# Attention and gated feed-forward on one core: products with v in one step, splits in four parts, first weights loaded earlier

## The chip, the cores and the metric

The kernel runs on one core of a Trainium2 chip. The metric is the device time of one execution in microseconds. Five engines work side by side, each through its own queue in order: TensorE (PE) multiplies and transposes, VectorE (DVE), ScalarE (ACT) and GpSimd (POOL) do the elementwise work, and SyncE (SP) issues most of the DMA transfers; POOL issues some itself. PEld in a profile is PE's loading of weights, which overlaps its multiplying.

## The reference

Two parts follow each other, all in float32:

```
scores = q k^T / 8 + bias[h]                 # 4 batches, 8 heads, 576 positions, 64 wide
bias   = relu(x w1 + b1) w2,  x = log1p(|i - j|) / log1p(max(i, 1))
attn   = softmax(scores);  out = attn v       # heads side by side: 2304 tokens x 512
h = out w_in                                  # 512 -> 2048
y = (h * tanh(softplus(h))) w_out             # 2048 -> 512
```

## The kernel before, in words

The bias stage comes first. It makes the bias for 16 positions at a time (36 tiles, `idx` 0 to 35), writes each tile to DRAM (`bias_d`), and reads whole bias blocks of a head pair back (`load_bias`).

The attention stage works through 16 pairs. A pair is one batch element with two heads, and it has five steps, one for each chunk of query rows in `ORDER = [0, 1, 4, 2, 3]`. Chunks 0 to 3 hold 128 rows of each head, chunk 4 the last 64 rows of both. `step(n)` writes the order of the work of step n by hand; n = 5i + x, with x the place in the pair. The work of a chunk is spread over several steps:

- `scores` (L218): q k^T in two PSUM tiles of 128x576. Each product is taken with q as a rounded high part (`hi`) and with the remainder (`q_lo`); the remainder of k lies in the lower half of `hi`.
- `add_bias` (L234, VectorE): adds the bias, finds the row extremes. `exps` (L249, ScalarE): exponential and row sums. For chunk 4 a 64-column copy follows on POOL (L252), which the last transpose of that chunk (L300) reads.
- `transposes` (L283 to L302), two steps later: PE turns the chunk, ScalarE copies it out of PSUM into `main` and `tail`. The PSUM tiles (`t_ps`) are three.
- `pv_duo(i, grp, k)` (L315 to L324): one of the five products with v of a group. Group 0 holds chunks 0 and 1, group 1 chunks 4, 2 and 3. The five add up in one PSUM tile `o`, of which there is one. VectorE copies it (L327) and SP stores it to `x_d` (L329 to L332).

The five products of a group are spread over three steps for group 0 (x = 4, then 0 and 1 of the next pair) and two for group 1 (x = 2 and 3 of the next pair), always behind the transposes of the step.

For the next pair, `load_hi` (L170, POOL's queue) loads q and k with rounding and `load_raw` (L161 to L164, SP's queue) loads them as they are, with v. `hi` has two buffers, raw has one. On POOL `split_k` (L175) and `split_q` (L180) subtract the one from the other, each as one instruction of 64x1216. Both loads are issued in the first step of the pair before.

Beside this the weights of the feed-forward part are loaded two at a time (`load_weights`, L105) and converted in four pieces each, L119 or L117, L122, L124 and L126, one or two pieces per step, mostly on VectorE. When a weight is done the next is loaded. For the first four weights POOL also does a subtraction (L137).

The feed-forward stage follows (L593 and L631): per block of tokens three passes of the first product, the gate, three passes of the second.

Of the kernel before, what the change touches and what calls it, by code (L numbers as in the profile page):

```python
# [7 lines left out]
F32 = mybir.dt.float32  # L8
# [3 lines left out]
ALU = mybir.AluOpType  # L12
# [3 lines left out]
B, H, S, D, C = 4, 8, 576, 64, 32  # L16
# [5 lines left out]
QW = 1216  # L22
# [24 lines left out]
def kernel(ctx: ExitStack, tc, qk, v, wb, w2, w_in, w_out, psia, psi4, rinv, eye, out):  # L47
# [122 lines left out]
        pool.dma_start(out=hi, in_=qk[b, hp])  # L170
        qk_hi[i] = hi

    def split_k(i):
        kl = qk_hi[i][64:128, QW:]
        (pool if i else dve).tensor_tensor(kl, qk_raw[i][64:128], kl.bitcast(F32), op=ALU.subtract)  # L175

    def split_q(i):

        lo = q_los[i % 2]
        (pool if i else dve).tensor_tensor(lo[0:64], qk_raw.pop(i)[0:64], qk_hi[i][0:64, :QW].bitcast(F32), op=ALU.subtract)  # L180
        q_lo[i] = lo

    def load_bias(hp, c):
# [55 lines left out]
    def exps(n, u):  # L239

        i, c = steps[n]
        if u == 1 and c == 4:
            return
        if i not in sums:
            sums[i] = st.tile([P, 9], F32, name="sums", bufs=3)
        pt, m = live[n]
        ps = pt[:, u * S:(u + 1) * S]
        k = 4 * u + c if c < 4 else 8
        act.activation(ps, ps, AF.Exp, bias=m[:, u:u + 1], scale=-1.0, accum_out=sums[i][:, k:k + 1])  # L249
        if c == 4:  # L250

            pool.tensor_copy(pt[:, S:640], pt[:, 512:S])  # L252

    def reciprocals(i):

# [48 lines left out]
    def pv_duo(i, grp, k):  # L304
        hp, b = divmod(i, B)
        main, tail = pt_t[i, grp]
        vt = v_t[i]
        w = 256 if grp == 0 else 320
        if k == 0:
            o_t[0] = o_ps.tile([P, 512], F32, name="o")  # L310
        o = o_t[0]
        kw = dict(skip_group_check=True)
        if k < 4:
            for h in range(2):
                pe.matmul(o[h * 64:h * 64 + 64, :w], vt[:, h, k, :], main[:, h, k, :],  # L315
                          start=(k == 0), stop=False, **kw)
            return
        if grp == 0:
            for h in range(2):
                pe.matmul(o[h * 64:h * 64 + 64, :w], vt[:, h, 4, :], tail, start=False, stop=True, **kw)  # L320
        else:
            pe.matmul(o[0:64, :w], vt[:, 0, 4, :], tail[:, 0:320], start=False, stop=True, **kw)
            pe.matmul(o[64:128, 64:320], vt[:, 1, 4, :], tail[:, 64:320], start=False, stop=True, **kw)
            pe.matmul(o[64:128, 0:64], vt[:, 1, 4, :], tail[:, 320:384], start=False, stop=True, **kw)  # L324
        del pt_t[i, grp]
        x = xs.tile([P, 320], F32, name="x")
        dve.tensor_copy(x[:, :w], o[:, :w])  # L327
        if grp == 0:
            sp.dma_start(out=x_d[b][:, hp, 0:256], in_=x[:, :256])  # L329
        else:  # L330
            sp.dma_start(out=x_d[b][:, hp, 256:512], in_=x[:, 64:320])
            sp.dma_start(out=x_d[b][:, hp, 512:576], in_=x[:, 0:64])  # L332
# [49 lines left out]
    def split(n):  # L382

        i, x = divmod(n, 5)
        if (x == 1 or n == 3) and i + 1 < NPAIR:
            split_k(i + 1)
        if x == 3 and i + 1 < NPAIR:
            split_q(i + 1)

        for _ in range((2, 2, 2, 1, 2)[x]):  # L390
            if not conv and w64:
                conv.append(conv_weights(x == 2))
            elif conv and next(conv[0]):
                conv.clear()
                load_weights()
                if w32[0][0] in order[:EARLY]:
                    split_weights(pool)

    def step(n):
        i, x = divmod(n, 5)  # L400
        late = n == 4

        def begin():
            if n < NS:
                scores(n)
                add_bias(n)
                exps(n, 0)

        def end():
            if n < NS:  # L410
                exps(n, 1)
                ahead(n)
            if 0 <= n - 1 < NS and (n - 1) % 5 == 4:
                rc[n - 1] = reciprocals((n - 1) // 5)
            if n < NS:
                split(n)


        if not late:
            begin()  # L420
        for k in {3: (0, 1)}.get(n, (n - LAG,)):
            if 0 <= k < NS:
                transposes(k)
        if not late:
            end()

        if late:
            for k in range(5):
                pv_duo(0, 0, k)
        for j, grp, ks in {4: ((i, 0, (0, 1)),), 0: ((i - 1, 0, (2, 3)),), 1: ((i - 1, 0, (4,)),),  # L430
                           2: ((i - 1, 1, (0, 1, 2)),), 3: ((i - 1, 1, (3, 4)),)}[x]:
            if 0 <= j < NPAIR and (j, grp) != (0, 0):
                for k in ks:
                    pv_duo(j, grp, k)
        if late:
            begin()
            end()

# [74 lines left out]
    for idx in range(NB + 2):  # L515
# [25 lines left out]
            load_raw(1)  # L541
        if idx == 18:
            load_hi(1)
    bias_scope.close()

    ptp = lsbuf("ptp", 1)
    xs = lsbuf("xs", 2)
    load_weights()
    x0 = lsbuf("x0")
    o_ps = lpsum("o_ps", 1)  # L550
    t_ps = lpsum("t_ps", 3)
# [105 lines left out]
    hidden(*units[0])  # L657
    step(NS + 1)
    step(NS + 2)
    step(NS + 3)  # L660
    left_scope.close()

    wq = sbuf("wq")
# [82 lines left out]
```

## Time and profile before

| what | value |
|---|---|
| median of 3 runs | 769.67 us (769.43 to 774.86) |
| the profiled execution | 776.47 us, its span 774.7 us |
| PE busy | 723.3 us, 93% of the span |
| VectorE, ScalarE, POOL busy | 68%, 59%, 14% |
| mean granted clock of PE | 0.977 |
| chain that ended last, by line | L631 and L593 24% each; load of raw q and k 4%; scores, products with v, bias loads 3% each |

The times are those of whole executions. A profile shows one execution, taken by itself; its span runs from its first to its last instruction, and its time is given beside it because sums over rows belong to that execution and not to the median. Busy shares are averages over stages with different limits: attention runs from about 60 to 357 us, the feed-forward stage from there to the end.

### The profile page before, as it was taken

What the parts mean: (1) busy time and instruction counts of PE and PEld (TensorE: products, weight loads), DVE (VectorE), ACT (ScalarE), POOL (GpSimd) and SP (SyncE); (2) the same over time, 40 slices, a digit from 0 to 9 for tenths busy, and PEclk for the clock granted to TensorE, in tenths of its full rate; (3) what the DMA queues carried; (4) which work ended last, traced back from release to release, by engine and by line L of the source; (5) the groups of instructions that cost most, each with busy time, mean ns of one, the idle gap of its engine ahead of it and who ended that gap; (6) DMA issues with size and microseconds to landing.
All of it is one profiled execution on the core that took longest, in us unless ns stands there. A gap on an engine that the chain in (4) does not pass through costs nothing.

```text
span 774.7 us, 11579 instructions
## 1 busy us (share of the span) xinstructions
PE 723.3 (93%) x4160; PEld 553.0 (71%) x4160; DVE 525.1 (68%) x1047; ACT 459.5 (59%) x982; POOL 110.9 (14%) x76
## 2 busy tenths in 40 slices
PE   6688989899988998979999999999999999999997
PEld 3226667676766676756888888888987888888886
DVE  7974788678857876744977856656557566665554
ACT  6986777677756776746766644444444554444443
POOL 1003443333332334350000000000000000000000
PEclk9989999999989999989999999999999999999999
DMA  8988469876975697820400003000410500010001
GB/s 280 297 282 278 121 207 316 211 238 189 320 213 165 200 320 227 252 52 16 117 1 2 0 20 90 0 1 1 129 35 1 136 0 1 1 55 1 1 0 55
DMA packets 45610, 93.60 MB, mean 121 GB/s; under 512 B 13408, under 2 KB 22256, under 8 KB 43504
## 3 DMA queue, kind: packets, MB, share of 16 engines
q1 hardware_dynamic: 42672, 72.70, 32.0%
q0 software_dynamic: 2304, 19.92, 7.8%
q8 instruction: 33, 0.54, 0.3%
q10 hardware_dynamic: 576, 0.22, 0.1%
q14 instruction: 25, 0.20, 0.1%
HBM read 72.43 MB, written 20.40 MB: 120 GB/s over the span
## 4 chain that ended last, share of the span: by engine, by line
PE 57%; DMA 16%; DVE 8%; ACT 5%; POOL 3%; issue 2%; SPq 2%; DVEq 0%; POOLq 0%; ACTq 0%
PE y L631 24%; PE h L593 24%; DMA rawqk<-in_qk_dram 4%; PE s L218 3%; PE o L315 3%; DMA bias<-bias_d 3%; DMA w<-in_w_out_dram 3%; DVE pt L234 2%; PE tp L283 2%; POOL qkhi L175 1%; ACT pt L249 1%; DMA w<-in_w_in_dram 1%; DMA vt<-in_v_dram 1%; ACT main L284 1%; DMA qkhi<-in_qk_dram 1%
## 5 line engine op out<-in xcount | busy, mean ns | idle before, releaser
L249 ACT ACTIVATE pt<-pt,m 128x576 f32<-128x576 f32 x144 | 112.8, 784 | 90.5 <-DVE m L234 90.5
L234 DVE CUSTOM_DVE_ANT_0 pt<-s,bias 128x576 f32<-128x576 f32 x144 | 103.8, 752 | 38.9 <-PE s L218 38.1
L631 PE MATMUL y<-who,ghi 128*128 128x512 f32 x288 | 113.8, 395 | 0.2 <-ACT ghi L615 0.2
L631 PE MATMUL y<-who,glo 128*128 128x512 f32 x288 | 113.9, 396 | 0.0
L631 PE MATMUL y<-wlo,ghi 128*128 128x512 f32 x288 | 113.7, 395 | 0.0
L615 ACT CAST ghi<-e 128x512 fp32r<-128x512 f32 x72 | 44.7, 621 | 89.9 <-DVE e L611 89.8
L315 PE MATMUL o<-main,vt 128*64 128x320 f32 (+1 forms) x512 | 79.8, 436 | 8.1 <-DVE x L327 8.0
L598 ACT ACTIVATE e<-h 128x512 f32<-128x512 f32 x72 | 42.9, 598 | 71.4 <-PE h L593 71.4
L218 PE MATMUL s<-qkhi 128*128 128x288 f32 x320 | 79.2, 330 | 3.9 <-issue 2.7
L599 DVE TENSOR_SCALAR e<-e 128x512 f32<-128x512 f32 x72 | 30.7, 426 | 76.2 <-ACT e L598 76.2
L593 PE MATMUL h<-xhi,whi 128*128 128x512 f32 (+1 forms) x320 | 81.0, 373 | 0.8 <-ACT xhi L575 0.7
L593 PE MATMUL h<-xlo,whi 128*128 128x512 f32 (+1 forms) x320 | 80.4, 372 | 0.9 <-DVE xlo L577 0.8
L593 PE MATMUL h<-xhi,wli 128*128 128x512 f32 (+1 forms) x320 | 80.0, 371 | 0.0
L616 DVE TENSOR_TENSOR glo<-e,ghi 128x512 fp32r<-128x512 f32 x72 | 49.7, 690 | 43.8 <-ACT ghi L615 43.8
L218 PE MATMUL s<-qkhi,qlo 128*128 128x288 f32 x320 | 71.0, 304 | 6.3 <-POOL qlo L180 6.3
L218 PEld LDWEIGHTS s<-qkhi 128*128 128x128 f32 x320 | 51.5, 195 | 32.5 <-issue 22.0
L283 PE MATMUL tp<-ident,pt 128*128 128x128 f32 x512 | 69.6, 281 | 1.0 <-ACT main L284 0.9
L284 ACT COPY main<-tp 128x512 f32<-128x512 f32 x128 | 67.7, 578 | 0.7 <-PE tp L283 0.5
L593 PEld LDWEIGHTS h<-xhi,whi 128*128 128x128 f32 x320 | 57.2, 188 | 14.1 <-ACT xhi L575 2.1
L593 PEld LDWEIGHTS h<-xlo,whi 128*128 128x128 f32 x320 | 56.8, 188 | 12.9 <-DVE xlo L577 1.7
L593 PEld LDWEIGHTS h<-xhi,wli 128*128 128x128 f32 x320 | 56.8, 188 | 11.3
L631 PEld LDWEIGHTS y<-who,glo 128*128 128x128 f32 x288 | 54.1, 188 | 13.7 <-DVE glo L616 0.9
(75 smaller groups left out, 1160.6 us busy)
## 6 DMA issues: line engine op xcount, KB each, us to landing
qkhi<-in_qk_dram POOLq DMA_DIRECT2D x16, 1216.0 KB, 7.7
bias_d<-bt SPq DMA_DIRECT2D x36, 295.5 KB
rawqk<-in_qk_dram SPq DMA_DIRECT2D x32, 304.0 KB
w<-in_w_in_dram SPq DMA_DIRECT2D x16, 512.0 KB
w<-in_w_out_dram SPq DMA_DIRECT2D x16, 512.0 KB
vt<-in_v_dram SPq DMA_DIRECT2D x16, 320.0 KB
bias<-bias_d SPq DMA_DIRECT2D x16, 288.0 KB
out_dram<-w SPq DMA_DIRECT2D x17, 256.0 KB
```

Of the source, the lines that this page charges most:

```text
L218: pe.matmul(s[:, j, :SH], stat[:, q0:q0 + P], hi[:, QW + kc + j * SH:QW + kc + (j + 1) * SH], start=(k == 0), stop=(k == len(todo) - 1))
L234: dve.tensor_tensor_reduce(out=halves(pt[:, sl]), in0=s[:, :, :SH], in1=halves(bt[:, sl]), scale=-0.125, scalar=BIG, op0=ALU.add, op1=ALU. ...
L249: act.activation(ps, ps, AF.Exp, bias=m[:, u:u + 1], scale=-1.0, accum_out=sums[i][:, k:k + 1])
L283: pe.transpose(tp[:, k * P:(k + 1) * P], pt[:, c0:c0 + P], ident)
L284: act.copy(main[:, h, :, off:off + P], tp.rearrange("p (k q) -> p k q", k=4))
L315: pe.matmul(o[h * 64:h * 64 + 64, :w], vt[:, h, k, :], main[:, h, k, :], start=(k == 0), stop=False, **kw)
L593: pe.matmul(h[:, u * n:(u + 1) * n], w["i", g4, d][:, r * P:(r + 1) * P], x[:, d, :n], start=(k == 0), stop=(k == 11))
L598: act.activation(e, h, AF.Exp)
L599: dve.tensor_scalar(e, e, E20, None, op0=ALU.min)
L615: act.copy(ghi, e)
L616: dve.tensor_tensor(glo, e, ghi.bitcast(F32), op=ALU.subtract)
L631: pe.matmul(ys[blk][t], g[:, c0:c0 + P], w, start=(f == 0 and k == 0), stop=(f == NFC - 1 and k == 2))
```

## The change: what it does

Five edits go together. (1) `step` runs the five products of a group in one step: group 0 at x = 4, group 1 at x = 2 of the next pair, the step after the last transposes of the group. They stand behind the scores and ahead of the transposes of that step; step 4, the first with products, keeps its own order. (2) VectorE's copy and the stores become a function of their own, `store_x`, at the end of that step. (3) From the second split on, `split_k` and `split_q` are four instructions of 64x304 each; their places in the program are x = 1 and 2 for k and x = 3 and 4 for q. (4) The 64-column copy of chunk 4 is made on ScalarE, behind its exponential. (5) The first call of `load_weights` stands at `idx` 26 of the bias stage.

```diff
--- before.py
+++ after.py
@@ -170,14 +170,21 @@
         pool.dma_start(out=hi, in_=qk[b, hp])
         qk_hi[i] = hi
 
-    def split_k(i):
-        kl = qk_hi[i][64:128, QW:]
-        (pool if i else dve).tensor_tensor(kl, qk_raw[i][64:128], kl.bitcast(F32), op=ALU.subtract)
-
-    def split_q(i):
+
+    QPART = QW // 4
+
+    def split_k(i, parts=range(4)):
+        for r in parts if i else (slice(0, QW),):
+            r = r if i == 0 else slice(r * QPART, (r + 1) * QPART)
+            kl = qk_hi[i][64:128, QW:][:, r]
+            (pool if i else dve).tensor_tensor(kl, qk_raw[i][64:128, r], kl.bitcast(F32), op=ALU.subtract)
+
+    def split_q(i, parts=range(4)):
 
         lo = q_los[i % 2]
-        (pool if i else dve).tensor_tensor(lo[0:64], qk_raw.pop(i)[0:64], qk_hi[i][0:64, :QW].bitcast(F32), op=ALU.subtract)
+        for r in parts if i else (slice(0, QW),):
+            r = r if i == 0 else slice(r * QPART, (r + 1) * QPART)
+            (pool if i else dve).tensor_tensor(lo[0:64, r], qk_raw[i][0:64, r], qk_hi[i][0:64, r].bitcast(F32), op=ALU.subtract)
         q_lo[i] = lo
 
     def load_bias(hp, c):
@@ -249,7 +256,7 @@
         act.activation(ps, ps, AF.Exp, bias=m[:, u:u + 1], scale=-1.0, accum_out=sums[i][:, k:k + 1])
         if c == 4:
 
-            pool.tensor_copy(pt[:, S:640], pt[:, 512:S])
+            act.copy(pt[:, S:640], pt[:, 512:S])
 
     def reciprocals(i):
 
@@ -323,6 +330,11 @@
             pe.matmul(o[64:128, 64:320], vt[:, 1, 4, :], tail[:, 64:320], start=False, stop=True, **kw)
             pe.matmul(o[64:128, 0:64], vt[:, 1, 4, :], tail[:, 320:384], start=False, stop=True, **kw)
         del pt_t[i, grp]
+
+    def store_x(i, grp):
+        hp, b = divmod(i, B)
+        w = 256 if grp == 0 else 320
+        o = o_t[0]
         x = xs.tile([P, 320], F32, name="x")
         dve.tensor_copy(x[:, :w], o[:, :w])
         if grp == 0:
@@ -382,10 +394,16 @@
     def split(n):
 
         i, x = divmod(n, 5)
-        if (x == 1 or n == 3) and i + 1 < NPAIR:
-            split_k(i + 1)
-        if x == 3 and i + 1 < NPAIR:
-            split_q(i + 1)
+        if i + 1 < NPAIR:
+            if n == 3:
+                split_k(1)
+                split_q(1)
+            elif i and x == 1:
+                split_k(i + 1, (0, 1))
+            elif i and x == 2:
+                split_k(i + 1, (2, 3))
+            elif i and x >= 3:
+                split_q(i + 1, ((0, 1), (2, 3))[x - 3])
 
         for _ in range((2, 2, 2, 1, 2)[x]):
             if not conv and w64:
@@ -416,25 +434,29 @@
                 split(n)
 
 
+        pv = [(j, grp) for at_x, j, grp in ((4, i, 0), (2, i - 1, 1)) if x == at_x and 0 <= j < NPAIR]
+
+        def products():
+            for j, grp in pv:
+                for k in range(5):
+                    pv_duo(j, grp, k)
+
+        def turn():
+            for k in {3: (0, 1)}.get(n, (n - LAG,)):
+                if 0 <= k < NS:
+                    transposes(k)
+
+
+        if late:
+            turn()
+            products()
+        begin()
         if not late:
-            begin()
-        for k in {3: (0, 1)}.get(n, (n - LAG,)):
-            if 0 <= k < NS:
-                transposes(k)
-        if not late:
-            end()
-
-        if late:
-            for k in range(5):
-                pv_duo(0, 0, k)
-        for j, grp, ks in {4: ((i, 0, (0, 1)),), 0: ((i - 1, 0, (2, 3)),), 1: ((i - 1, 0, (4,)),),
-                           2: ((i - 1, 1, (0, 1, 2)),), 3: ((i - 1, 1, (3, 4)),)}[x]:
-            if 0 <= j < NPAIR and (j, grp) != (0, 0):
-                for k in ks:
-                    pv_duo(j, grp, k)
-        if late:
-            begin()
-            end()
+            products()
+            turn()
+        end()
+        for j, grp in pv:
+            store_x(j, grp)
 
 
 
@@ -541,11 +563,12 @@
             load_raw(1)
         if idx == 18:
             load_hi(1)
+        if idx == 26:
+            load_weights()
     bias_scope.close()
 
     ptp = lsbuf("ptp", 1)
     xs = lsbuf("xs", 2)
-    load_weights()
     x0 = lsbuf("x0")
     o_ps = lpsum("o_ps", 1)
     t_ps = lpsum("t_ps", 3)
@@ -657,7 +680,6 @@
     hidden(*units[0])
     step(NS + 1)
     step(NS + 2)
-    step(NS + 3)
     left_scope.close()
 
     wq = sbuf("wq")
```

How the order on the engines changes shows in three places. PE before, from the third step of a pair (first row) through its fifth: `s` are scores, `tp` transposes, `o` products, and 952 is the group 1 of the pair before, 1096 group 0 of this pair.

```order
L218 MATMUL s<-qkhi,qlo_117 128x288 x2
L283 MATMUL tp<-ident,pt 128x128 x8
L286 MATMUL tp<-ident,pt 128x128
L315 MATMUL o<-main_952,vt 64x320 x6
L218 MATMUL s<-qkhi 128x288 x2
...
L286 MATMUL tp<-ident,pt 128x128
L315 MATMUL o<-main_952,vt 64x320 x2
L322 MATMUL o<-tail_953,vt 64x320
...
L300 MATMUL tp<-ident,pt_1092 128x128
L315 MATMUL o<-main_1096,vt 64x256 x4
L218 MATMUL s<-qkhi 128x288 x2
```

The same stretch of PE in the changed kernel (958 is group 1 of the pair before, 1115 group 0 of this pair):

```order
L225 MATMUL s<-qkhi,qlo_117 128x288 x2
L322 MATMUL o<-main_958,vt 64x320 x8
L329 MATMUL o<-tail_959,vt 64x320
...
L290 MATMUL tp<-ident,pt 128x128 x8
...
L225 MATMUL s<-qkhi,qlo_117 128x288 x2
L322 MATMUL o<-main_1115,vt 64x256 x8
L327 MATMUL o<-tail_1116,vt 64x256 x2
L303 MATMUL tp<-ident,pt_1099 128x128 x4
L307 MATMUL tp<-ident,pt_1099 128x128
L225 MATMUL s<-qkhi 128x288 x2
```

All products of a group now stand between the scores and the transposes of one step, and none are left for the steps after it. The second place is POOL, one split and the load behind it, before:

```order
L175 TENSOR_TENSOR qkhi<-rawqk,qkhi 64x1216
L252 COPY pt_1535<-pt_1535 128x64
L180 TENSOR_TENSOR qlo_116<-rawqk,qkhi 64x1216
L170 DMA qkhi<-in_qk_dram 128x2432
L175 TENSOR_TENSOR qkhi<-rawqk,qkhi 64x1216
```

and in the changed kernel:

```order
L180 TENSOR_TENSOR qkhi<-rawqk,qkhi 64x304 x4
L187 TENSOR_TENSOR qlo_116<-rawqk,qkhi 64x304 x4
L170 DMA qkhi<-in_qk_dram 128x2432
L180 TENSOR_TENSOR qkhi<-rawqk,qkhi 64x304 x4
L187 TENSOR_TENSOR qlo_117<-rawqk,qkhi 64x304 x4
```

The copy is gone from POOL, and the load still stands behind the last part. The third place is SP, from the stores of one group 1 to the next raw load, before (`rawqk` is raw, `r_d` the reciprocals of the row sums):

```order
L329 DMA x_d_83<-x 128x256
L105 DMA w_1782<-in_w_out_dram 128x1024
L331 DMA x_d_83<-x 128x256
L332 DMA x_d_83<-x 128x64
L161 DMA rawqk<-in_qk_dram 64x1216
```

and in the changed kernel:

```order
L105 DMA w_1821<-in_w_out_dram 128x1024
L343 DMA x_d_83<-x 128x256
L344 DMA x_d_83<-x 128x64
L341 DMA x_d_80<-x 128x256
L161 DMA rawqk<-in_qk_dram 64x1216
```

The store of group 0 of the running pair (L341) now stands directly ahead of the raw load, where before the stores of group 1 of the pair before stood.

## Rows read from the trace of the kernel before

**Rows 1.** View by stretches: PE, PEld, DVE, ACT, POOL busy, granted clock, DMA share, GB/s.
```profile
60.00:350.00 290.00, 262.74 (x1856) 198.49 (x1856) 206.19 (x465) 197.63 (x512) 107.39 (x68) 0.95 0.73 219
400.00:425.00 25.00, 25.00 (x109) 20.12 (x108) 19.67 (x34) 16.49 (x29) 0.00 (x0) 1.00 0.00 1
```

**Rows 2.** Waits of PE in 60 to 350: total us, times, longest.
```profile
PE tp L300 <- POOL pt L252: 8.8, 5, 3.2
PE o L315 <- DVE x L327: 7.1, 10, 2.7
PE s L218 <- POOL qlo L180: 6.3, 5, 3.8
PE s L218 <- issue: 2.7, 1, 2.7
```

**Rows 3.** Timeline of POOL, one ordinary turn: start, us, line, [idle before].
```profile
147.53 0.57 POOL L170 DMA_DIRECT2D qkhi<-in_qk_dram  x1
158.28 2.79 POOL L175 TENSOR_TENSOR qkhi<-rawqk,qkhi 64x1216 fp32r<-64x1216 f32 x1 [10.18 <-DMA rawqk<-in_qk_dram]
161.13 0.24 POOL L252 COPY pt<-pt 128x64 f32<-128x64 f32 x1
161.32 2.79 POOL L180 TENSOR_TENSOR qlo<-rawqk,qkhi 64x1216 fp32r<-64x1216 f32 x1
164.06 0.57 POOL L170 DMA_DIRECT2D qkhi<-in_qk_dram  x1
```

**Rows 4.** Timeline of POOL: first and last of twelve issues, and two prices.
```profile
76.43 1.28 POOL L137 TENSOR_TENSOR wli<-w,whi 128x512 fp32r<-128x512 f32 x1 [7.59 <-ACT whi L136]
...
109.72 0.57 POOL L170 DMA_DIRECT2D qkhi<-in_qk_dram  x1
...
124.36 0.58 POOL L252 COPY pt<-pt 128x64 f32<-128x64 f32 x1
...
314.00 0.57 POOL L170 DMA_DIRECT2D qkhi<-in_qk_dram  x1
```

**Rows 5.** Waits of all engines in 60 to 350.
```profile
POOL qkhi L175 <- DMA rawqk<-in_qk_dram: 128.2, 11, 14.7
```

**Rows 6.** Timeline, late turns: POOL and PE.
```profile
215.93 2.74 POOL L175 TENSOR_TENSOR qkhi<-rawqk,qkhi 64x1216 fp32r<-64x1216 f32 x1 [14.71 <-DMA rawqk<-in_qk_dram]
...
219.10 0.33 PE L300 MATMUL tp<-ident,pt 128*128 128x128 f32 x1 [3.19 <-POOL pt L252]
...
337.21 0.85 PE L218 MATMUL s<-qkhi,qlo 128*128 128x288 f32 x2 [3.79 <-POOL qlo L180]
```

**Rows 7.** Timeline of DVE, PE and POOL around 235.
```profile
231.69 3.17 DVE L124 SCALAR_TENSOR_TENSOR w<-w,w 128x512 uint32<-128x512 uint32 x1
...
235.24 1.84 PE L315 MATMUL o<-main,vt 128*64 128x320 f32 x12 [2.69 <-DVE x L327]
...
236.90 0.24 POOL L252 COPY pt<-pt 128x64 f32<-128x64 f32 x1 [2.59 <-ACT pt L249]
...
242.12 0.57 POOL L170 DMA_DIRECT2D qkhi<-in_qk_dram  x1 [2.25 <-PE s L218]
```

**Rows 8.** View by stretches: the clock after two stalls.
```profile
70.00:74.00 4.00, 3.38 (x16) 3.39 (x17) 3.93 (x13) 2.64 (x7) 0.00 (x0) 0.57 0.94 352
335.00:345.00 10.00, 7.79 (x39) 6.30 (x40) 4.02 (x9) 3.30 (x8) 4.65 (x3) 0.66 0.23 53
```

**Rows 9.** Chain of waits (start, us), timeline of DVE and PE: first weights.
```profile
63.80 5.27 DMA w<-in_w_in_dram
...
69.09 0.43 DVE L119 TENSOR_SCALAR w<-w 128x512 f32<-128x512 f32 x1 [7.44 <-DMA w<-in_w_in_dram]
...
70.62 0.82 PE L218 MATMUL s<-qkhi 128*128 128x288 f32 x2 [2.66 <-issue]
```

**Rows 10.** Timeline of PE: products of group 0 in three places.
```profile
168.10 1.08 PE L315 MATMUL o<-main,vt 128*64 128x256 f32 x8
...
171.46 0.65 PE L320 MATMUL o<-tail,vt 128*64 128x256 f32 x4
```

## The prediction

> **What bounds the kernel now.** The first view to read is the one by stretches. It cuts the program in two. In 400 to 425 TensorE (PE) is busy for 25.00 of 25.00 us: the feed-forward part is bound by PE, its work and order stay as they are, and it is worth nothing here. In 60 to 350, the attention part, PE is busy for 262.74 of 290 us, so it idles for 27.3, and its granted clock is 0.95, which takes another 5% of 290, or 14.5 us [rows 1]. Together 42 us is the most that any reordering of attention can give.
>
> The view of waits says who ends those idle times [rows 2]: 8.8 us for the 64-column copy that POOL makes in the third chunk of a pair (L252), 7.1 us for VectorE's copy of the products out of their one PSUM buffer (L327), 6.3 us for POOL's split of q (L180), and one gap of 2.7 us marked "issue". Three of the four are touched by the change, so 18.6 us look like a sure gain.
>
> The third view, POOL's timeline, says why they are not. One turn of POOL reads [rows 3]: issue of the load of the next pair's q and k (147.53), wait of 10.18 for the second, raw copy of them, split of k (2.79), the small copy, split of q (2.79), and at once the next issue (164.06). There is one raw buffer, so the next raw load needs this split's end as well. **This is a loop of its own**: load, split, load. From the first to the last of the twelve issues from 109.72 to 314.00 there are eleven turns in 204.28 us, 18.57 each [rows 4]. Of each, 0.57 is the issue, the wait for raw is 128.2 / 11 = 11.65 on average [rows 5], and 6.35 are left for the splits and what stands between them. So where PE waits for POOL, PE is waiting for this loop. The turn at 215.93 shows it: raw lands 14.71 us after POOL came free, and only then can the copy follow for which PE has been idle 3.19 us [rows 6]. Take the copy out of POOL and PE arrives at the scores of the next pair and waits there for q, on the same chain.
>
> **The change part by part.**
>
> *Copy L252 goes to ScalarE.* It was 0.24 us on POOL, 0.58 where VectorE held it up [rows 3, 4]. On ScalarE it stands right behind the exponential that writes its input, so the wait of 8.8 us goes. What is late next is the split of q. I count nothing for it beyond the POOL time below, except in the last turn.
>
> *Products all in one step.* No product is added; the five of a group move in front of the step's transposes. What it gives is slack: the PSUM buffer is now copied in the third and the fifth step of a pair and wanted again two steps on, so the 7.1 us go too. Their largest is the 2.69 us at 235.24, behind a VectorE shift-and-or that took 3.17 us while POOL split k [rows 7]. In that turn PE's lateness did reach the loop: the issue at 242.12 waited 2.25 us for PE to let go of the buffer. That wait I take as gained: **-2.25**. The other nine lie in turns that the loop sets anyway.
>
> *Splits in four parts.* 128x512 takes 1.28 us and 64x1216 takes 2.79 [rows 3, 4], so a column costs (2.79 - 1.28) / 704 = 2.14 ns and an instruction 0.18 us. A part of 304 columns is an estimated 0.83 us and eight are 6.66, against 5.78 from the start of k's split to the next issue in the ordinary turn [rows 3] and 6.35 on average, a mean that holds the copy, its waits and its hold-ups. I take 6.66 - 6.35 = 0.31 more per turn, in eleven turns **+3.4**. Bounds: with no cost per instruction eight parts take 5.2, 1.15 less per turn; with a hold-up of 0.58 - 0.24 = 0.34 at each of the six new boundaries they take 8.7, 2.35 more. In return PE needs only five of eight parts for the first half of the first scores and seven for the second, and VectorE is held for one part, not 2.79.
>
> *The loads.* Each turn waits 11.65 on average for raw and 10.18 in the ordinary one. The stores of the products move from the fourth and second step of a pair to its third and fifth: that of group 1 leaves earlier, while POOL splits and the loads pause, and that of group 0 now stands on SP directly ahead of the next raw load. VectorE's conversions, which release the weight loads on SP, are held for less. I take a third of the 1.47 between mean and ordinary, 0.5 per turn, **-5.5**; bounds 0 and -16.
>
> *First weights 10 tiles earlier.* [...] The two loads take 5.27 us [rows 9] and now go ahead of bias rows that the third and fourth chunk read back: bounds from -7.4 (what VectorE waits) to +0.9 (all 5.27 lands on the path).
>
> *The last turn.* Raw is late again and PE stands for 3.79 us before 337.21 [rows 6], then runs 10 us at 0.66, which costs 3.4 [rows 8]. The products that used to come after this stall, 1.08 + 0.65 = 1.73 us [rows 10], come before it now, and I give half of the clock's loss back: **-3.4**.
>
> Sum: -2.25 + 3.4 - 5.5 - 4.4 - 3.4 = -12.2 us. The profiled execution took 776.47, so it would take 764.3. The median of the runs is 6.8 lower; I subtract the same from it: 769.67 - 12.2 = **757.5**.
>
> **The rivals.** One per cent, 7.7 us, is about what can be told from no change: faster means under 762.0, slower over 777.4.
>
> *PE sets the pace after all.* If the loop has room (turns with 10.18 of wait and 5.2 to 6 of splits are 16 to 17 us), PE gains what its own waits hold: 8.8 + 7.1 + 2.7 and two thirds of the clock's 14.5, which is 28.3, and 741 comes out. For it: at 242.12 POOL waits for PE. Against it: eleven waits for raw with a mean of 11.65.
>
> *A store takes the place of the wait.* On SP the store of group 0 waits for a VectorE copy that is queued behind two conversion pieces; the raw load stands behind it. If raw leaves as late as today, the -5.5 is gone (763); if it leaves another 0.5 later per turn, 768.5. I put this at **766**. The change then does what it says and nothing comes of it. For it: a conversion piece can take 3.17 us [rows 7], and it would now lie in front of the load.
>
> [...] VectorE's pieces and POOL's splits hold each other up: 3.17 us beside a split, 0.58 for a copy of 0.24 [rows 4, 7]. With eight short instructions POOL has six more places at which to be late. At 0.34 each this is 2.04 per turn and 22.4 in eleven turns; 757.5 + 22.4 = **780**. It decides from splits of some 8.5 us per turn on. [...]
>
> **How the numbers follow.** Forecast (750 to 764 around 757.5) 0.47; PE sets the pace (741) 0.15; the store (766) 0.27; POOL (780) 0.11. Faster: nearly all of the first two, 0.58. Same: the store, the forecast's upper end and a mild form of POOL, 0.30. Slower: 0.12. The range of 8 in 10 leaves out most of POOL and half of the PE case: 744 to 770.
>
> **What the profile of the changed kernel would show.** The waits for L252 and for the product copy gone from PE's list; the wait for q's parts larger than 6.3 or about equal, since it takes over. POOL: parts near 0.83 us, eight of them in 6.2 to 7.2. VectorE: no conversion piece over 1.5 us in attention. The turn: 18.57 falling to some 18.2. No wait of 7 us for the first weights, and the clock at 1.00 around 70. Wrong would be: turns under 17.5 (then PE set the pace), eight parts in over 8 us, raw issued later behind the store, or a new wait of PE for ScalarE's copies, since the products now stand only one block of scores behind the transposes that feed them.

## The result, and the profile after

The changed kernel takes **781.54 us** (median of 20 runs, 774.85 to 786.31) where the kernel before, run beside it, takes 774.98 (20 runs). The ratio is **1.0094 [1.0071, 1.0118]**: about 7 us slower, and the prediction said 12.2 faster.

Its profiled execution took 774.85, its span 772.6. It is the shortest of its runs, 6.7 below its median, and also shorter than the 776.47 of the one profiled before. So the two profiles, laid beside each other, can't show where 7 us were lost; what they show is which waits went and which came. The loss has to be found by taking the edits apart.

View by stretches, changed kernel (columns as in [rows 1]); the last two lines answer to [rows 8]:

```profile
60.00:350.00 290.00, 261.88 (x1889) 211.47 (x1890) 192.20 (x470) 203.87 (x532) 118.56 (x134) 0.97 0.74 217
400.00:425.00 25.00, 25.00 (x109) 20.14 (x108) 19.70 (x33) 16.35 (x29) 0.00 (x0) 1.00 0.00 1
70.00:74.00 4.00, 3.70 (x28) 3.03 (x27) 3.97 (x13) 2.91 (x8) 0.00 (x0) 1.00 0.94 349
335.00:345.00 10.00, 9.75 (x55) 8.44 (x57) 4.58 (x13) 6.57 (x16) 4.73 (x5) 0.71 0.13 33
```

The feed-forward stretch is what it was. In attention PE is still busy for 262 of 290 us: the waits changed their names, not their sum. POOL's busy time rose from 107.39 to 118.56, although a copy was taken from it and the first split now lies ahead of this stretch. The clock around 70 is now 1.00 instead of 0.57.

Waits of PE, and those of POOL and ScalarE that bear on them, 60 to 350 (columns as in [rows 2]; L225 is `scores`, L187 `split_q`, L322 the products, L291 ScalarE's copy of the transposes, L117 a weight conversion on ScalarE):

```profile
POOL qkhi L180 <- DMA rawqk<-in_qk_dram: 136.2, 13, 13.2
...
PE s L225 <- POOL qlo L187: 11.7, 13, 3.3
...
PE o L322 <- ACT main L291: 9.7, 7, 3.5
ACT w L117 <- DMA w<-in_w_out_dram: 9.7, 3, 3.9
...
PE s L225 <- DVE m L241: 4.0, 9, 1.0
```

Against [rows 2]: the waits for the 64-column copy (8.8) and for VectorE's copy of the products (7.1) are gone as forecast. In their place stand the wait for q's parts, 11.7 in 13 places where it was 6.3 in 5, and a new one of 9.7 for ScalarE's copies of the transposes. POOL waits for raw as before (136.2 in 13 places; the view of before has 128.2 in 11 and puts one more, of 12.1, down to ScalarE).

Timeline of POOL, changed kernel: one ordinary turn, the first and last of twelve issues, and four parts that nothing held up (answers to [rows 3, 4]):

```profile
106.93 0.57 POOL L170 DMA_DIRECT2D qkhi<-in_qk_dram  x1
...
144.28 0.57 POOL L170 DMA_DIRECT2D qkhi<-in_qk_dram  x1
155.85 3.37 POOL L180 TENSOR_TENSOR qkhi<-rawqk,qkhi 64x304 fp32r<-64x304 f32 x4 [11.00 <-DMA rawqk<-in_qk_dram]
159.29 4.08 POOL L187 TENSOR_TENSOR qlo<-rawqk,qkhi 64x304 fp32r<-64x304 f32 x4
163.31 0.57 POOL L170 DMA_DIRECT2D qkhi<-in_qk_dram  x1
...
314.08 0.57 POOL L170 DMA_DIRECT2D qkhi<-in_qk_dram  x1
...
334.08 3.18 POOL L187 TENSOR_TENSOR qlo<-rawqk,qkhi 64x304 fp32r<-64x304 f32 x4
```

The turn is (314.08 - 106.93) / 11 = 18.83 us, against 18.57. From the start of k's split to the next issue it takes 163.31 - 155.85 = 7.46, where the ordinary turn of before took 5.78. Four unhindered parts are 3.18, so 0.80 each, and a whole split 2.79: the instruction itself costs about what the prediction worked out (0.83). Read over all eleven turns, each timed in the same way, the load part (issue to start of k's split) and the split part are:

| last eleven turns of the profile, us per turn | turn | load | split |
|---|---|---|---|
| before | 18.57 | 12.10 | 6.47 |
| changed kernel | 18.83 | 11.59 | **7.24** |

The last issue falls at 314.08, where it was at 314.00; the 2.8 us won up to the first ordinary issue (106.93 instead of 109.72) are used up by eleven turns that are 0.26 longer.

Timeline of ScalarE and of PE around 158, changed kernel, for the new wait:

```profile
157.45 0.66 ACT L117 ACTIVATE w<-w 128x512 f32<-128x512 f32 x1 [3.88 <-DMA w<-in_w_out_dram]
...
158.77 1.05 ACT L291 COPY main<-tp 128x512 f32<-128x512 f32 x2
...
159.39 2.89 PE L322 MATMUL o<-main,vt 128*64 128x256 f32 x12 [3.47 <-ACT main L291]
```

ScalarE stands 3.88 us for a weight that is still being loaded, with the copy behind it that the products want. In the kernel before ScalarE waited so for 3.3 us in two places, and no product waited for its copies; now the products stand one block of scores behind the transposes that feed them.

### The profile page after: what moved, and what is told of

Read it like the earlier page. It is cut to its first block, busy times and chain, and to the rows that moved or that the text cites. A ratio compares the mean times of both kernels' runs of the same rounds, so it can differ in the third digit from the quotient of the medians.

```text
span 772.6 us, 11588 instructions
## 1 busy us (share of the span) xinstructions
PE 720.0 (93%) x4160; PEld 564.2 (73%) x4160; DVE 512.3 (66%) x1047; ACT 463.9 (60%) x998; POOL 139.3 (18%) x150
## 4 chain that ended last, share of the span: by engine, by line
PE 60%; DMA 17%; DVE 5%; ACT 5%; POOL 4%; SPq 2%; issue 1%; DVEq 0%; ACTq 0%; POOLq 0%
PE h L616 24%; PE y L654 24%; PE o L322 5%; DMA w<-in_w_out_dram 4%; DMA rawqk<-in_qk_dram 4%; DMA bias<-bias_d 3%; PE s L225 3%; POOL qkhi L180 2%; POOL qlo L187 2%; PE tp L290 2%; ACT pt L256 2%; DVE pt L241 2%; DMA xr<-r_d 2%; DMA bias_d<-bt 1%; DMA qkhi<-in_qk_dram 1%
## 5 line engine op out<-in xcount | busy, mean ns | idle before, releaser
L241 DVE CUSTOM_DVE_ANT_0 pt<-s,bias 128x576 f32<-128x576 f32 x144 | 103.9, 751 | 43.4 <-PE s L225 43.4
L180 POOL TENSOR_TENSOR qkhi<-rawqk,qkhi 64x304 fp32r<-64x304 f32 x60 | 62.5, 1067 | 174.5 <-DMA rawqk<-in_qk_dram 167.0
L322 PE MATMUL o<-main,vt 128*64 128x320 f32 (+1 forms) x512 | 83.1, 423 | 10.8 <-ACT main L291 9.7
L225 PE MATMUL s<-qkhi,qlo 128*128 128x288 f32 x320 | 70.9, 304 | 11.8 <-POOL qlo L187 11.7
L225 PE MATMUL s<-qkhi 128*128 128x288 f32 x320 | 77.0, 322 | 5.0 <-DVE m L241 4.0
L291 ACT COPY main<-tp 128x512 f32<-128x512 f32 x128 | 68.4, 587 | 7.5 <-PE tp L290 7.3
L322 PEld LDWEIGHTS o<-main,vt 128*64 128x64 f32 x512 | 44.3, 139 | 37.5 <-ACT main L291 20.3
```

The source lines that it names most:

```text
L180: (pool if i else dve).tensor_tensor(kl, qk_raw[i][64:128, r], kl.bitcast(F32), op=ALU.subtract)
L225: pe.matmul(s[:, j, :SH], stat[:, q0:q0 + P], hi[:, QW + kc + j * SH:QW + kc + (j + 1) * SH], start=(k == 0), stop=(k == len(todo) - 1))
L241: dve.tensor_tensor_reduce(out=halves(pt[:, sl]), in0=s[:, :, :SH], in1=halves(bt[:, sl]), scale=-0.125, scalar=BIG, op0=ALU.add, op1=ALU. ...
L291: act.copy(main[:, h, :, off:off + P], tp.rearrange("p (k q) -> p k q", k=4))
```

## The experiments

Each was timed against the kernel before on the same chip. "Before" there ran at 771.71 to 773.14 us. Three sets of runs were made, and ratios of different sets are compared through that kernel. Ratios under 1 are faster.

### The parts alone taken back: undo_parts

The splits are whole and stand where they stood (k's alike); the other four edits stay.

```diff
-        for r in parts if i else (slice(0, QW),):
-            r = r if i == 0 else slice(r * QPART, (r + 1) * QPART)
-            (pool if i else dve).tensor_tensor(lo[0:64, r], qk_raw[i][0:64, r], qk_hi[i][0:64, r].bitcast(F32), op=ALU.subtract)
+        (pool if i else dve).tensor_tensor(lo[0:64], qk_raw.pop(i)[0:64], qk_hi[i][0:64, :QW].bitcast(F32), op=ALU.subtract)
```

> The changed kernel with both splits whole again, at their old places; the other edits stay. If the parts lengthened the load loop, the turns of POOL (18.8 us in the changed kernel) fall: splits take 5.8 to 6 us instead of 7.2, so 1.2 us less in each of fourteen turns, and the ratio to the kernel before is about 0.99 (767 where before is 775). If the products' new places cost the time, the ratio stays at about 1.01 and the wait of PE for ScalarE's copies (9.7 us) is still there.

Measured: 764.39 us, **0.9888 [0.983, 0.9945]**. The interval lies far from the 1.0094 of the changed kernel; the difference of the two ratios, 0.0206, is 16 us. Timeline of POOL in this kernel, first and last of twelve issues and two turns:

```profile
109.11 0.57 POOL L170 DMA_DIRECT2D qkhi<-in_qk_dram  x1
...
142.77 2.75 POOL L176 TENSOR_TENSOR qkhi<-rawqk,qkhi 64x1216 fp32r<-64x1216 f32 x1 [14.81 <-DMA rawqk<-in_qk_dram]
145.59 2.83 POOL L181 TENSOR_TENSOR qlo<-rawqk,qkhi 64x1216 fp32r<-64x1216 f32 x1
148.38 0.57 POOL L170 DMA_DIRECT2D qkhi<-in_qk_dram  x1
157.44 2.78 POOL L176 TENSOR_TENSOR qkhi<-rawqk,qkhi 64x1216 fp32r<-64x1216 f32 x1 [8.49 <-DMA rawqk<-in_qk_dram]
160.29 3.15 POOL L181 TENSOR_TENSOR qlo<-rawqk,qkhi 64x1216 fp32r<-64x1216 f32 x1
...
307.94 0.57 POOL L170 DMA_DIRECT2D qkhi<-in_qk_dram  x1
```

The first of the two turns has a split part of 148.38 - 142.77 = 5.61, the mean of eleven is 5.91; the turn is 198.83 / 11 = 18.08. Where the 1.33 per turn between 7.24 and 5.91 comes from is in the view of groups by line and shape, POOL, 75 to 345 (busy time, then mean ns of one), the first two lines of the changed kernel:

```profile
L187 POOL TENSOR_TENSOR qlo<-rawqk,qkhi 64x304 fp32r<-64x304 f32 x56 | 51.6, 949 | 1.0
L180 POOL TENSOR_TENSOR qkhi<-rawqk,qkhi 64x304 fp32r<-64x304 f32 x56 | 49.0, 900 | 143.7 <-DMA rawqk<-in_qk_dram 136.2 <-DMA qkhi<-in_qk_dram 7.4
```

and of this one:

```profile
L181 POOL TENSOR_TENSOR qlo<-rawqk,qkhi 64x1216 fp32r<-64x1216 f32 x14 | 41.4, 2961 | 0.8
L176 POOL TENSOR_TENSOR qkhi<-rawqk,qkhi 64x1216 fp32r<-64x1216 f32 x14 | 39.3, 2806 | 149.8 <-DMA rawqk<-in_qk_dram 141.4 <-DMA qkhi<-in_qk_dram 8.4
```

100.6 us in 14 turns against 80.7: the parts cost POOL 19.9. Without any hold-up 112 parts are 112 x 0.795 = 89.0 and 28 whole splits of 2.76 are 77.3, so 11.7 is the price of more instructions, 0.84 per turn. The rest, 8.2 or 0.59 per turn, is hold-up: the parts lost 11.6 to it, whole splits 3.4. Together that is 1.42 per turn over these 14 turns, 1.33 over the last eleven.

Not all of it reaches the turn. The load part is 0.58 shorter with parts, so the turn is only 0.75 longer; eleven times that is 8.3 us, of the 9.1 between the two profiled executions (774.85 and 765.73). That the ratios stand 16 us apart and not 9 fits the changed kernel's profile being its fastest run; no profile of it near its median is on record.

### The parts alone: only_parts

The kernel before with edit (3) as its only one.

> The kernel before with the splits in four parts as the only edit. If the parts cost 1.3 us in each of fourteen turns by themselves, the ratio is 1.015 to 1.02. If they cost only together with the new places of the products, it is 1.00.

Measured: 780.24 us, **1.0116 [1.0084, 1.0148]**; turn 19.00, split part 7.64, and PE waits 16.3 us in 16 places for q's parts. That is less than the 1.015 to 1.02 expected, but slower both alone and among the others: the loss belongs to the parts.

### Two parts in place of four: halves

```diff
-    QPART = QW // 4
+    QPART = QW // 2
```

and the tables of parts to match: k's halves at x = 1 and 2, q's at x = 3 and 4.

> The changed kernel with each split in two parts of 608 columns at the same places, instead of four. If the price is one per boundary, from an instruction's own cost and from VectorE slipping in, two of the six added boundaries are left: splits take 5.9 + 0.44 = 6.35 us, and the ratio is a third of the way from 0.989 to 1.009: 0.995. If the price comes from splitting at all or from the places in the order, it is 1.005 or more.

Measured: 769.1 us, 0.996 [0.9932, 0.9988]; split part 6.21. Split part and time lie between those of whole splits (5.91, 0.9888) and of four parts (7.24, 1.0094), though the interval overlaps that of whole splits. So the price goes with the number of boundaries, and not with splitting at all or with the places in the order.

### A second raw buffer: parts_raw2 and whole_raw2

The loop load, split, load rests on the one raw buffer. A second one lets the load leave before the split ends.

```diff
-    rawp = rsbuf("raw", 1, side="right")
+    rawp = rsbuf("raw", 2, side="right")
```

In the changed kernel:

> The changed kernel with two buffers for raw q and k instead of one, nothing else: the next raw load no longer needs the end of this split. If the loop of load and split sets the time, the wait for raw (11.0 us per turn) falls towards that for the rounded load (7.5 to 9), turns of 18.8 us come near 17, and the ratio to the kernel before falls from 1.009 to 0.99 or lower although the splits still take 7.2. If the parts cost their time in another way (VectorE, PE's order), the ratio stays at 1.009.

and in the one with whole splits:

> Whole splits at their old places, the other edits of the change, and two raw buffers. If the loop still set the time with whole splits (ratio 0.989), this falls further, to about 0.975. If PE sets it by then, it stays at 0.985 to 0.99.

Measured with four parts: 767.49 us, **0.9938 [0.9913, 0.9962]**, against 1.0094 with one buffer; turn 17.95, though the split part stays long (7.34). POOL's wait for raw in 60 to 350 falls from 136.2 to

```profile
POOL qkhi L180 <- DMA rawqk<-in_qk_dram: 80.2, 8, 12.1
POOL qkhi L180 <- DMA qkhi<-in_qk_dram: 51.2, 6, 9.6
```

The second line is the wait for the rounded load, 7.4 in the changed kernel, which now ends last in six places: the two together fall from 143.6 to 131.4, and the turn by 0.88, not to the 17 expected. So the long split part costs as much as it does because it stands in the loop. With whole splits: 764.36 us, 0.9892 [0.985, 0.9935], no different from undo_parts with one buffer. Once the splits are short, a second buffer gives nothing that this measurement tells; the profile's shorter turn there (17.27) did not show in the median.

### The other edits taken back one at a time, parts left in

undo_products puts the products and their stores back at their old places (three steps for group 0, two for group 1):

```diff
-            products()
-            turn()
-        end()
-        for j, grp in pv:
-            store_x(j, grp)
...
+        for j, grp, ks in {4: ((i, 0, (0, 1)),), 0: ((i - 1, 0, (2, 3)),), 1: ((i - 1, 0, (4,)),),
+                           2: ((i - 1, 1, (0, 1, 2)),), 3: ((i - 1, 1, (3, 4)),)}[x]:
+            if 0 <= j < NPAIR and (j, grp) != (0, 0):
+                for k in ks:
+                    pv_duo(j, grp, k)
+                    if k == 4:
+                        store_x(j, grp)
```

> The changed kernel with the products back at their old places over three and two steps; parts, copy and weights stay. If the products' new places cost the time (9.7 us of waits of PE for ScalarE's copies, and the clock after them), the ratio to the kernel before falls to about 0.995 and those waits go. If the loop with its parts sets the time, the ratio stays at 1.01 and the turns stay at 18.8 us.

undo_weights calls `load_weights` after the bias stage again:

```diff
-        if idx == 26:
-            load_weights()
...
+    load_weights()
```

> The changed kernel with the first weights loaded after the bias stage again. If the early load is the gain that was forecast for it, this is 4 us slower than the changed kernel (ratio 1.014 to 1.015) and VectorE waits 7 us for the weights again. If the early load only moved the bias rows back by as much, the ratio stays at 1.01 and the third bias block is read 2 us earlier than in the changed kernel (64.5).

undo_copy makes the 64-column copy on POOL:

```diff
-            act.copy(pt[:, S:640], pt[:, 512:S])
+            pool.tensor_copy(pt[:, S:640], pt[:, 512:S])
```

> The changed kernel with the 64-column copy back on POOL. Then POOL holds the second pair's split back until the attention stage, as in the kernel before. If the split that now runs inside the bias stage costs time there (VectorE's last 17 pieces took 9.4 us instead of 6.5), the bias stage ends 2 to 3 us earlier and the ratio is about 1.006. If it does not, the copy's wait comes back on PE and the ratio is 1.01 to 1.02.

| taken back | time | ratio | turn | load | split |
|---|---|---|---|---|---|
| products | 777.79 | 1.0055 [1.0018, 1.0092] | 18.73 | 11.54 | 7.20 |
| first weights | 781.83 | 1.0101 [1.0035, 1.0167] | 19.26 | 12.08 | 7.17 |
| copy | 780.99 | 1.0105 [1.0053, 1.0158] | 19.42 | 11.83 | 7.59 |

None differs from the changed kernel (1.0094) by more than the intervals hold, the products' the most. With the parts in place all three keep a split part over 7 us, and all are slower than before. Two signs that were expected did not come. Without the early weights VectorE waits 8.7 us for them again and the time is the same, though the third bias block is read at 66.08, not earlier than 64.51. With the copy back on POOL no wait of PE for it is left, and the ratio is still 1.0105.

### The other edits with whole splits

Four more kernels, all with whole splits: copy and weights (the products at their old places), products and copy, products and weights, and products alone. Their edits are those shown above. The recorded text of the last calls its weights early; they stand at their old place there, and nothing but the products is changed, so it can't serve as the repeat that the text speaks of.

> The kernel before with the copy on ScalarE and the first weights early; splits whole, products at their old places. Theory (with whole splits the gain of 0.989 is the products' new place, since the raw load and PE's waits for VectorE's copy depend on it): about 0.997 of before, split time per POOL turn near 5.7 to 5.9 as the copy is gone, turn near 18.4. Rival (the copy out of POOL makes the gain, 0.35 us to 0.6 us of every turn of the loop): 0.989 to 0.991, turn near 18.1.

> The changed kernel with whole splits and without the early weights: products together and copy on ScalarE remain. Theory (early weights give nothing that lasts, as taking them out of the changed kernel moved it from 1.0094 to 1.0101): 0.989, as with them. Rival (the early weights gain the 4.4 us of the prediction once the parts no longer hide it): 0.9945.

> The changed kernel with whole splits and the 64-column copy back on POOL: products together and early weights remain. Theory (products make most of the gain; the copy adds 0.35 to 0.6 us to each turn of the loop, 5 to 8 us in all): 0.995 to 1.0, split time per turn back near 6.4. Rival (the copy is nothing to the time): 0.989.

> The changed kernel with whole splits, copy on POOL and early weights, run again beside the others as only_products was built with the weights early: see prod_weights; the two should agree within 0.3 per cent. If they differ by more, differences of that size between kernels of this study can't be read.

| with whole splits | time | ratio | turn | load | split |
|---|---|---|---|---|---|
| products, copy, weights (undo_parts) | 764.39 | 0.9888 [0.983, 0.9945] | 18.08 | 12.17 | 5.91 |
| products, weights | 763.64 | **0.9878 [0.9839, 0.9917]** | 17.93 | 11.94 | 5.99 |
| products | 765.42 | 0.9903 [0.9866, 0.9941] | 17.68 | 11.72 | 5.97 |
| products, copy | 769.0 | 0.9945 [0.991, 0.9979] | 18.01 | 12.12 | 5.89 |
| copy, weights | 768.24 | 0.996 [0.9924, 0.9997] | 18.05 | 11.96 | 6.09 |

The products' new place alone makes the kernel 1.0% faster, and without it the other two come to 0.4%. The copy adds nothing on top: split parts of 5.97 and 5.99 with it on POOL, 5.89 and 5.91 without, and the times are, if anything, better with it there, though these intervals overlap. The weights give 0.0057 with the copy on ScalarE and 0.0025 with it on POOL, 4.4 and 1.9 us; these intervals overlap too. The version with products and weights is the fastest of all that ran by its median, not told apart from undo_parts or from the products alone.

Six pairs of kernels now differ in the parts alone:

| edits beside the parts | ratio with parts | with whole splits | difference | longer turn, times 11 | between the profiled executions |
|---|---|---|---|---|---|
| products, copy, weights | 1.0094 | 0.9888 | 0.0206 | 8.3 us | 9.1 us |
| products, weights | 1.0105 | 0.9878 | 0.0227 | 16.4 | 18.6 |
| products, copy | 1.0101 | 0.9945 | 0.0156 | 13.8 | 14.8 |
| copy, weights | 1.0055 | 0.996 | 0.0095 | 7.5 | 8.4 |
| none | 1.0116 | 1 | 0.0116 | 4.7 | 2.5 |
| products, copy, weights, second raw buffer | 0.9938 | 0.9892 | 0.0046 | 7.5 | 8.0 |

In each pair the longer turn accounts for what lies between the two profiled executions to within 2.3 us (kernels of different sets are compared there as they are, and "before" differs by up to 3.3 us between the sets): the parts cost their time in POOL's loop. How much they cost depends on the other edits. With one raw buffer it is 1 to 2%, most where the products moved; there whole splits gain what parts then take away.

Why moving the copy does not help the start is seen in the bias stage, where POOL's first split now slips in, since the copy that waited for attention no longer stands ahead of it. View by stretches of 34 to 41 (DVE is the third pair of numbers, POOL the fifth), first the products alone, where POOL is idle there as before:

```profile
34.00:41.00 7.00, 4.22 (x53) 0.92 (x44) 7.00 (x24) 6.26 (x16) 0.00 (x0) 0.93 1.00 340
```

then products and copy, with two whole splits there:

```profile
34.00:41.00 7.00, 2.83 (x34) 0.67 (x26) 7.00 (x9) 4.46 (x11) 5.32 (x2) 0.88 1.00 333
```

then the changed kernel, where the parts start:

```profile
34.00:41.00 7.00, 4.10 (x56) 0.88 (x46) 7.00 (x24) 6.20 (x16) 6.10 (x2) 1.00 0.87 313
```

Under whole splits VectorE gets 9 instructions done in place of 24, and ScalarE 11 in place of 16; the first load of the loop leaves at 72.04 in place of 67.33. Under parts VectorE keeps its 24, and it is POOL that stands: one of k's four parts takes 10.99 us, the other three 0.82 to 0.99. It began 0.01 us behind the first of 32 VectorE pieces, and the next part began only when these were through. Then the sides change: q's parts take 0.92 each, and of VectorE's 17 pieces from 47.26 on the five beside POOL's parts take 1.01 to 1.03 in place of 0.46, so that the 17 stretch to 9.41 us. Timelines of POOL and DVE, changed kernel; the second line is the long part alone, out of the four of the first:

```profile
34.90 13.52 POOL L180 TENSOR_TENSOR qkhi<-rawqk,qkhi 64x304 fp32r<-64x304 f32 x4 [30.80 <-DMA rawqk<-in_qk_dram]
35.69 10.99 POOL L180 TENSOR_TENSOR qkhi<-rawqk,qkhi 64x304 fp32r<-64x304 f32 x1
48.49 3.68 POOL L187 TENSOR_TENSOR qlo<-rawqk,qkhi 64x304 fp32r<-64x304 f32 x4
...
35.68 10.30 DVE L518 TENSOR_SCALAR ht<-at,bb 128x304 f32<-128x304 f32 x32
...
47.26 9.41 DVE L518 TENSOR_SCALAR ht<-at,bb 128x448 f32<-128x448 f32 x17
```

With POOL idle there, in the kernel with the products alone, the 32 take as long, and the same 17 take less:

```profile
35.60 10.30 DVE L506 TENSOR_SCALAR ht<-at,bb 128x304 f32<-128x304 f32 x32
...
47.18 6.52 DVE L506 TENSOR_SCALAR ht<-at,bb 128x448 f32<-128x448 f32 x17
```

## Why the prediction was wrong

*What bounds the kernel* was right as far as it was tried. In the changed kernel the second raw buffer shows it: with the split part as long as before (7.34), 1.5% comes back. In the kernel before it was not tried. PE's waits for the copy and the products went, and the wait for q grew on the same chain.

*Splits in four parts, +3.4.* **This is the step that failed.** The price of one part was right (0.83 worked out, 0.80 measured). What it was set against was not: 6.66 for eight parts without a hold-up was compared with 6.35 for two splits with the copy, its waits and their hold-ups in it. The 6.35 is itself 6.47 when each turn is timed (the 128.2 holds a wait behind the last issue, 13.4, and lacks one of 12.1 that the view puts down to ScalarE). Of it, two waits of one turn (2.59 and 2.25, [rows 7]) are 0.44, and they go with the copy's or the products' edit; the 2.25 even stands in the sum twice, as a gain of its own and inside the mean. With whole splits the part is 5.97 where the products alone moved and 5.91 with all other edits, and that is what the eight parts have to be set against: 0.75 more per turn where 0.31 stood. The hold-ups at the new boundaries, which had been a bound and not the value, add the rest: 7.24 measured, 0.58 above 6.66. In place of +3.4 the parts cost 16 us by the ratios among the other edits, and 9 us (0.0116 of 771.71) alone.

*The rival at 780*, a hold-up of POOL at each boundary, had this mechanism, at 0.11. Its price of 2.04 per turn, all hold-up, was too much; about 0.6 is hold-up and 0.84 the instructions themselves. That its 780 lies beside 781.54 is in part luck: it was counted from gains of 15.6 us that came to 8.7. It was to decide from 8.5 us of splits per turn on; 7.24 were enough, because the other gains were smaller as well.

*The loads, -5.5.* In the profile the load part did fall by 0.51 per turn, 12.10 to 11.59, the 0.5 of the forecast. But it is no gain of the stores' new place: with that and whole splits it is 12.17, so the shorter load part comes with the parts and is already inside their 16. What the traces show is when SP issues the raw load, on the mean of the eleven turns behind POOL's issue: 1.76 us before, 0.93 in the changed kernel, 0.49 in only_parts. That fits the prediction's other reason, conversions held for less. The stores' new place works against it: raw leaves 0.43 us later with parts (0.50 in undo_products) and 0.68 later with whole splits (2.45 in undo_parts, 1.77 in copy_weights), the half microsecond that the rival of the store had named. One turn each of timelines of POOL and SP, first the changed kernel, whose POOL issue at 163.31 is shown above, then undo_parts:

```profile
164.42 0.32 SPq L341 DMA_DIRECT2D x_d<-x  x1
164.84 0.48 SPq L161 DMA_DIRECT2D rawqk<-in_qk_dram  x1
...
164.22 0.57 POOL L170 DMA_DIRECT2D qkhi<-in_qk_dram  x1 [0.77 <-PE s L219]
166.94 0.36 SPq L335 DMA_DIRECT2D x_d<-x  x1
167.40 0.47 SPq L161 DMA_DIRECT2D rawqk<-in_qk_dram  x1
```

The load part does not follow this delay alone (12.08 in undo_weights, with 0.68 of delay); what else sets it was not tried.

*Copy L252, nothing.* It gave nothing in the loop, as said; the first split's move into the bias stage was not seen ahead.

*Products, -2.25, and the last turn, -3.4.* The products alone give 0.0097 of 772.25, 7.5 us, with an interval from 4.6 to 10.3. That holds the two terms' 5.65; which place brought how much was not taken apart. In the profile of that kernel the turn is 17.68 against 18.57, so the gain is also in the loop, where the prediction had counted one turn. The clock of the last turn, over 325 to 350, is 0.86 in the kernel before and in copy_weights; with the products moved and whole splits it is 0.88 (products alone), 0.98, 1.00 and 1.00, and in the changed kernel 0.86 again. So as far as one profile of each tells, the clock's part of the gain came with whole splits, and the parts took it away.

*First weights, -4.4.* This is PE's gap of 2.66 [rows 9] and, for the clock of 0.57 over 4 us [rows 8], (1 - 0.57) x 4 = 1.7; no run shows a gain of 4.4 that stands clear of its interval. The wait of 7.44 [rows 9] is gone, and the clock around 70 is 1.00. Timeline of DVE in the changed kernel:

```profile
61.39 0.08 DVE L241 DVE_READ_ACCUMULATOR2_ANT m<- 128x1 f32 x1
61.39 0.44 DVE L119 TENSOR_SCALAR w<-w 128x512 f32<-128x512 f32 x1
```

The conversion starts as soon as VectorE gets there. Yet with parts in the loop the time is the same without this edit (1.0101 against 1.0094); with whole splits it is worth 1.9 to 4.4, and these intervals do not tell that from nothing.

*The sum.* Forecast -12.2, measured about +7.3 (0.0094 of 774.98). Of the 19.5 between, 12.6 are the parts (16 in place of 3.4). The other terms were to give -15.6 and give 0.0112 of 773.14, -8.7, which is the remaining 6.9; most of that would be the 5.5 of the loads, of which the kernel with whole splits shows nothing.

*The signs.* Right: the waits for the copy and the products gone, q's wait larger than 6.3, parts near 0.83, the first weights' wait and the clock. No conversion piece is over 1.5 us (the longest 1.41), where 3.17 stood. Wrong: eight parts in 6.2 to 7.2 (7.24), and the turn at 18.2 (18.83). Of the signs named for a failure, raw issued later behind the store did not come (0.93 us behind POOL's issue, where it was 1.76). The last one came, a new wait of PE for ScalarE's copies, 9.7 us. It falls to 5.5 in parts_raw2 and to 1.9 in undo_parts; ScalarE waits 5.5 and 0.8 for weights there, in the changed kernel 9.7. Why the weights come later under parts was not settled.

## What to carry to other kernels

When several edits touch one engine, price each against the state that the others leave, not against the mean of the profile before, in which their savings still stand. Splitting POOL's instructions gave VectorE 20.7 us here and cost POOL 19.9; before splitting one, find out which of the two engines stands in the loop that sets the time. Here VectorE, the busier of the two, had time to spare (busy for 206 of the 290 us of attention before). POOL was busy for 14% of the span before and had none, since its splits stand between one load and the next.

## What the runs showed of the hardware

POOL's subtractions and some of VectorE's elementwise work held each other up in these runs. In the kernel before, over 75 to 345, a conversion piece of L122 takes 1.60 us in the mean where it overlaps one of POOL's splits (9 pieces) and 0.43 where it does not (22); in the changed kernel it takes 0.81 (8) and 0.42 (23), and POOL's parts take 0.90 and 0.95 in place of 0.80. Three of VectorE's conversion pieces, 75 to 345, undo_parts:

```profile
L126 DVE SCALAR_TENSOR_TENSOR w<-w,w 128x512 uint32<-128x512 uint32 x32 | 33.9, 1058 | 0.5
L124 DVE SCALAR_TENSOR_TENSOR w<-w,w 128x512 uint32<-128x512 uint32 x31 | 26.3, 849 | 0.4
L122 DVE TENSOR_SCALAR w<-w 128x512 uint32<-128x512 uint32 x31 | 25.1, 810 | 0.0
```

and the changed kernel:

```profile
L126 DVE SCALAR_TENSOR_TENSOR w<-w,w 128x512 uint32<-128x512 uint32 x31 | 24.7, 797 | 0.5
L124 DVE SCALAR_TENSOR_TENSOR w<-w,w 128x512 uint32<-128x512 uint32 x31 | 23.7, 763 | 0.4
L122 DVE TENSOR_SCALAR w<-w 128x512 uint32<-128x512 uint32 x31 | 16.2, 522 | 5.9 <-DMA w<-in_w_out_dram 5.9
```

85.3 us against 64.6: the parts give VectorE 20.7 us (1.1 of it a piece less in the stretch) and cost POOL 19.9. That the two are alike does not mean that one engine gets what the other loses: of POOL's 19.9, 11.7 are the price of more instructions, and 8.2 are hold-up. Not everything on VectorE was held: its sums of scores and bias (L241) have a mean of 751 ns in the changed kernel, for the 52 that overlap one of POOL's parts as for the 75 that do not.

Which of the two stood was not told by the length of POOL's instruction alone. In the bias stage whole splits ran at 2.76 and 2.74, as if alone, and VectorE stood; here is q's split with the piece that began 0.02 us behind it, from the timelines of products and copy:

```profile
38.44 2.74 POOL L181 TENSOR_TENSOR qlo<-rawqk,qkhi 64x1216 fp32r<-64x1216 f32 x1
38.46 2.89 DVE L506 TENSOR_SCALAR ht<-at,bb 128x304 f32<-128x304 f32 x1
```

Such a piece takes 0.36 us at the start of this row in the changed kernel (35.68 to 36.04). In the same stage of the changed kernel it is the other way round: the part that began 0.01 us behind the first of 32 pieces took 10.99 us in place of 0.80, and lost 10.2 us to a row of pieces that kept their pace, 10.30 us for the 32 as in the kernel where POOL is idle there. From 47.43 on, parts and pieces take turns: a part takes 0.86 to 0.99 us, and a piece beside it some 1.02 in place of 0.46.

The part of 10.99 us waited for more than the piece ahead of it: that one ended at 36.04, and 31 pieces that had begun after the part went ahead of it. Each of them began some 0.07 us before the piece ahead of it ended; whether that is why the part had to wait for the whole row was not tried.
